# Attention and channel mixing in one kernel: first batch mixed 256 columns wide, its first hidden tile by channel tile, the last product's end in two parts, and a new order of all steps

## The chip, the core and the metric

The kernel runs on one core of one Trainium2 chip. The time is the device time of one execution in microseconds (us), as a median of several runs. Five engines work side by side: PE (TensorE, matrix products; its weight loads are listed apart as PEld), DVE (VectorE), ACT (ScalarE), POOL (GpSimd) and SP (SyncE, which here issues every DMA). Each engine works through its own list of instructions in order and waits on semaphores for the others.

## The reference

Four batches of 768 tokens, 8 heads of 64 channels. Each token attends to its neighbours nearer than 16 and to 24 block summaries (the maximum of the keys, the mean of the values over 32 tokens); the result `x` is mixed over tokens by a product of rank 32 and then goes through two channel products.

```python
scores_l = scale * q @ k^T          # kept where |i - j| < 16
scores_s = scale * q @ k_sum^T + log(32)
a = softmax(concat([scores_l, scores_s]))
x = a @ concat([v, v_sum])          # (4, 768, 512)
u = x + (x^T @ U @ V)^T             # U: 768 x 32, V: 32 x 768
out = u + relu(u @ w_ch1) @ w_ch2   # 512 -> 2048 -> 512
```

## The kernel before, in words

**Front.** Nothing of the channel products can start before batch 0 has been through its attention. Per head the steps are: load keys (`lk`, line 310), queries (`lq`, line 324) and, for two heads at once, values (`lv`, line 345); block maxima on DVE (`K`, line 418) and their copies into the key tile; scores on PE (line 474); masked exponentials on DVE and ACT (lines 499, 509); transposes on PE (line 583) and their copies (line 589); the means of four heads' values on PE (`M`, line 399) and eight copies of them into the value tiles (line 437); the product with the values (line 599); the division on DVE (`N`, lines 627 to 629), which writes `x`. The second `M` (heads 4 to 7) needs the last of the value loads.

Then `x` is mixed. A channel tile is 128 channels (two heads), there are four. `I` (line 642) multiplies `x` by `U` for two channel tiles, as 12 matmuls of 128 columns that use the four 32-column strips of the array in turn; `J` (line 660) adds up the strips by a product with `rep`; both results are copied (lines 655, 668, 670). `G` (`mix_u`) turns three token tiles of one channel tile (three transposes, line 676) and adds the mixed part to the same bank (line 684); `Go` splits the sum into a rounded part on ACT (line 714) and the rest on DVE (line 715). A half is 384 tokens, so there are eight `G`. The hidden tile `f` of half `hf` is `up` (line 1015): 12 matmuls, three for each of four channel tiles.

**Weights.** They come as 64-bit words: a load of 512 KB (`la`, `lb`, `W`, line 802), a scaling on ACT (line 244), three turning steps (POOL line 264, DVE lines 270 and 273), and a split into two parts (ACT line 288, DVE or POOL line 289).

**Main stream.** After the front PE does one group of matmuls after the other: for batch 0 `up` and `down_rows` (line 1037) in turn, for batches 1 to 3 products of half-size blocks (lines 1300, 1396, 1498). The attention of the next batch, the weights and the outputs are laid between these groups. In the batches after the first the exponentials take a way through DRAM before the product with the values (line 613): `s` sends them (line 534), `f` fetches them in four pieces (line 542), `v` loads the values (lines 338, 339).

**Order.** The order of the whole program is the string `PLAN`: words, each one step, with "/" after which the next group of main matmuls follows. What stands before the first "/" is the front (its words begin with a dot). The same order holds on every engine's list, SP's too, and each load's place on SP's list is the place of its word. `.w4` puts four matmuls of 128x120 on a tile of zeros into PE's list (`keep_busy`, line 1139).

**End.** The last stage is 56 pairs of groups of six matmuls of 384 columns (line 1498). After the last group DVE adds the result to `u` (line 1524), and SP sends it (line 1529).

Of the kernel before, what the change touches and what calls it, by code (L numbers as in the profile page):

```python
# [18 lines left out]
P = 128  # L19
BLOCK, WIN = 32, 16  # L20
NB = S // BLOCK
NU = S // P
# [45 lines left out]
    .lu .li .X .w4 .z1 .w4 .lk0 .lk3 .K0 .Xt0 .Kd0 .lq0 .lm .lq3 .lk2 .K3 .S0 .Kd3 .S3 .m .K2  # L68
    .Kp2 .E0.2 .w4 .lq2 .E0.1 .lk1 .F .w4 .lq1 .E1.0 .E7.0 .E6.2 .E1.1 .lv0 .S2 .lv1 .E0.0 .E1.2
    .T1 .K1 .E7.2 .Xt1 .T0 .E7.1 .C0 .E6.1 .lk7 .C1 .E5.2 .E5.0 .E6.0 .Kp1 .E5.1 .lk6 .w4 .T7  # L70
    .S1 .T5 .Xt2 .E2.0 .E4.1 .E2.1 .lq7 .T6 .E3.0 .lq6 .lq4 .M0 .E3.2 .E2.2 .E3.1 .Mo0 .Dp0
    .E4.0 .lk4 .K7 .Kp7 .lk5 .T2 .Bp1 .T3 .C6 .E4.2 .C5 .K6 .Bp0 .C7 .S7 .Kd6 .V1 .C2 .lv2 .T4
    .Dp3 .Xs .Bp3 .V0 .V7 .K4 .E15.2 .lq5 .Kp4 .Dp2 .E14.2 .E15.1 .V6 .C3 .N3 .E15.0 .E14.1 .lv3
    .S6 .Xl .C4 .la0 .S4 .K5 .Qs .E14.0 .Bd2 .Dp1 .E8.1 .V5 .E13.0 l1.0.0 .Kp5 .V4 .E8.2 .N0 .S5
    .E12.2 .E8.0 .V3 .V2 .E11.1 .E13.1 .E12.0 .M1 .lr .E9.0 .E12.1 .E11.2 .T12 .E13.2 .E11.0
    .E9.1 .T8 .T15 .Mo1 .Z0 .C12 .C15 .Dp6 .E10.2 .E10.1 .la1 .Qf .E10.0 .N1 .N2 .T13 .lb0 .T14
    .I0 .Y0.0 .T11 .E9.2 .Bd6 .Dd5 .T9 .Io0 .C11 .Bp4 .Bp7 .C13 .la2 .C8 .Y0.1 .Dp4 .V12 .lb1
    .C9 .V11 .V13 .Y0.2 .J0 .lb2 .V8 .N6 .la4 .Bp5 .T10 a1.0.0 .la3 .V9 .C14 .V14 .Jo0 .C10 q1.0
    .V10 .Dp7 .N4 k1.0 .G0.0 .V15 .G0.1 .lb3 .N5 .Z1 .N7 .Go0.0 a1.0.0 .G1.1 .Go0.1 .I2 .G1.0
    .Y1.0 .Io2 .J2 .z0 .w4 .Y1.1 .Jo2 .G0.2 .W0 .G0.3 .Y1.2 .Go0.2 l1.0.1 .Go0.3 .Z2 .G1.2  # L80
    .Go1.1 .Go1.2 a1.0.0 t2 W0.5 .G1.3 a1.0.0 .Go1.0 t2 .Go1.3 .U0.0 .W1 a1.0.0 / / / t2 c0.4 t2
    t2 a1.0.0 K1.0 .lb4 t2 c0.3 t3 a1.0.0 a1.0.1 w0.0 c1.2 / l1.1.0 w0.1 / x1.1 t3 x0.2 t3 v1.1
    D1 Ka1.0 v1.0 / c1.3 k1.1 S1.0.1 / E1.0.1.0 E1.0.1.1 W0.6 E1.0.1.2 S1.0.0 t3 a1.0.1 t4
    E1.0.0.1 t3 c0.5 E1.0.0.0 D0 K1.1 t5 a1.0.1 E1.0.0.2 a1.0.1 t3 Ka1.1 x0.3 w1.0 / T1.0 x1.2
    q1.1 k1.2 K1.2 / / c1.4 S1.1.0 a1.0.1 t4 / E1.1.0.2 W1.5 U0 S1.1.1 E1.1.0.0 a1.1.0 E1.1.0.1
    W1.6 s1.0 Ka1.2 q1.2 U1 w1.1 E1.1.1.2 E1.1.1.0 t4 a1.0.1 D2 E1.1.1.1 t4 k1.3 Us0 t4 t4 t5 t5
    Us1 f1.0 / c1.5 U4 a1.0.1 a1.0.1 x1.3 / D3 x0.4 a1.0.1 c0.6 / W0.7 t6 S1.2.0 t5 Ba1.1.1 U3
    T1.1 W0.8 E1.2.0.1 Ba1.0.0 E1.2.0.0 a1.1.0 E1.2.0.2 / t5 s1.1 t5 / q1.3 x0.5 W1.7 t6 x1.4
    a1.1.0 D4 S1.2.1 W0.9 Ba1.0.1 E1.2.1.1 K1.3 f1.1 E1.2.1.2 / E1.2.1.0 t6 / t6 c0.7 c0.8 P1.0
    Ba1.1.0 t6 / c1.6 W1.8 N1.0 T1.2 w2.0 t7 Ka1.3 t8 k1.4 / S1.3.0 / s1.2 E1.3.0.2 E1.3.0.0  # L90
    S1.3.1 t6 E1.3.0.1 q1.4 c1.7 P1.1 w2.1 k1.5 x1.5 E1.3.1.0 E1.3.1.1 t7 v1.2 E1.3.1.2 N1.1
    K1.4 x0.6 t7 T1.3 Ka1.4 / Ba1.2.1 / t7 v1.3 c1.8 q1.5 t7 w3.0 t7 / S1.4.0 Ba1.2.0 x1.6 U5
    f1.2 D5 E1.4.0.2 W1.9 R1.0 c0.9 t8 K1.5 x0.7 E1.4.0.0 w3.1 l1.1.1 t8 / Ba1.3.1 W0.10 / /
    E1.4.0.1 W0.11 S1.4.1 Ba1.3.0 E1.4.1.0 E1.4.1.2 E1.4.1.1 a1.1.0 t8 P1.2 t9 s1.3 t9 N1.2 t8
    t8 / / x1.7 T1.4 W1.10 x0.8 q1.6 Ka1.5 c0.10 U6 / a1.1.1 S1.5.0 t10 / f1.3 a1.1.0 E1.5.0.2
    S1.5.1 D7 W1.11 D6 E1.5.0.1 c1.9 t9 t10 E1.5.0.0 t9 t9 c0.11 k1.6 a1.1.1 E1.5.1.1 c1.11 t10
    U7 t11 t9 r1.0 / s1.4 a1.1.0 W0.12 E1.5.1.0 a1.1.1 t10 x1.8 / a1.1.0 g1.0 a1.1.1 E1.5.1.2
    t10 K1.6 Ka1.6 P1.3 N1.3 x0.9 c0.12 / a1.1.1 a1.1.1 M1.0 t10 Mo1.0 c1.10 / J1.0 R1.1 t11 D8
    t11 k1.7 a1.1.1 Jo1.0 x0.10 K1.7 / O1.0.0 W0.13 Us2 x1.9 / t11 t11 Us3 t11 t12 / / f1.4
    c0.13 U2 T1.5 S1.6.0 w5.0 U10 a1.1.1 x0.11 w4.0 / r1.1 t12 E1.6.0.1 q1.7 D10 / E1.6.0.2 v1.4  # L100
    t12 E1.6.0.0 w5.1 a1.1.1 x1.10 W1.12 / S1.6.1 g1.1 U11 W0.14 t13 D9 / U9 W1.13 v1.6 E1.6.1.0
    c1.12 E1.6.1.2 Ba1.4.1 t12 E1.6.1.1 Ka1.7 t12 t13 O1.0.1 t12 w4.1 x0.12 / s1.5 Ba1.4.0 t13
    O1.0.1 O1.0.1 / O1.0.2 P1.4 Us4 t13 x1.11 O1.0.1 t13 c0.14 N1.4 W0.15 / U8 W1.15 T1.6 v1.5
# [87 lines left out]
def body(ctx: ExitStack, tc, q0, q1, k, v, vn, uv, w1, w2, mask, ident, rep, out):  # L191
# [1473 lines left out]
```

## Time and profile before

| | |
|---|---|
| median of 3 runs | 625.55 us (622.32 to 626.25) |
| the profiled execution | 626.52 us, of it the span from first to last instruction 624.3 us |
| PE busy | 610.4 us, 98% of the span |
| DVE, ACT, POOL busy | 72%, 56%, 55% of the span |
[...]
| start of the first `up` / of the first `down_rows` on PE | 50.25 us / 54.55 us |
| end of the last matmul | 620.82 us |

All views are of this one execution; times in them are from the start of its span. A busy PE is not PE at its peak: the ends of matmuls are modelled, so a pause shorter than a matmul does not show as idle.

### The profile page before, as it was taken

To read this page: it belongs to the slowest core of one execution; us is meant where nothing else is said; L and a number is where in the kernel's file an instruction comes from. 1 tells how busy PE (TensorE), PEld (TensorE's weight loads), DVE (VectorE), ACT (ScalarE), POOL (GpSimd) and SP (SyncE) were. 2 spreads that over 40 slices of the span, in tenths; PEclk is the share of its full clock that TensorE was granted. 3 is DMA by queue.
4 is the path that set the end of the run, shared out by engine and by line. 5 is a ranking of instruction groups with operands and counts; after the bars stand their busy time and mean duration, and the time that the engine had idled before them with its cause. 6 is when DMAs were issued, how large, how long until landed. Compare 5 with 4: busy or idle time off the path is not lost.

```text
span 624.3 us, 14694 instructions
## 1 busy us (share of the span) xinstructions
PE 610.4 (98%) x5376; PEld 557.9 (89%) x5376; DVE 446.5 (72%) x1139; ACT 350.9 (56%) x794; POOL 345.6 (55%) x393
## 2 busy tenths in 40 slices
PE   7899999999999999999999999999999999999997
PEld 6679989889987999988887899998888899999997
DVE  5689768678888766779787764776557553579992
ACT  3776666563653666665544556675463556767620
POOL 5377964786666687785345677654333575640000
PEclk9999999999999999999999999999999999999999
DMA  8997998999968678799896786687879645455443
GB/s 222 230 323 246 285 313 258 288 291 325 295 197 281 226 239 262 241 301 300 262 305 181 210 266 203 198 256 237 253 242 311 220 133 168 149 191 203 145 119 126
DMA packets 97559, 148.30 MB, mean 238 GB/s; under 512 B 9680, under 2 KB 67920, under 8 KB 97488
## 3 DMA queue, kind: packets, MB, share of 16 engines
q1 hardware_dynamic: 97488, 147.38, 76.4%
q8 instruction: 42, 0.69, 0.5%
q14 instruction: 29, 0.24, 0.1%
HBM read 104.67 MB, written 42.66 MB: 236 GB/s over the span
## 4 chain that ended last, share of the span: by engine, by line
PE 81%; DMA 12%; SPq 3%; DVE 1%; issue 1%; ACT 1%; POOL 1%; DVEq 0%; ACTq 0%
PE ps_h L1300 25%; PE acc L1396 17%; PE ps_h L1015 10%; PE acc L1037 10%; PE accx L1498 4%; PE accy L1498 3%; PE accz L1498 3%; DMA place<-in_k 2%; PE ps_x L613 2%; DMA dsum<-tmp 2%; PE ps_s L474 2%; PE ps_s L451 2%; DMA there<-squares 2%; SPq L542 1%; DMA whole<-up 1%; DMA place<-in_v 1%
## 5 line engine op out<-in xcount | busy, mean ns | idle before, releaser
L967 POOL TENSOR_TENSOR parts<-whole,parts 128x512 fp32r<-128x512 f32 (+1 forms) x128 | 159.3, 1258 | 77.3 <-ACT parts L963 72.9
L1300 PE MATMUL ps_h<-place,parts 128*128 128x384 f32 x1008 | 179.5, 336 | 0.7 <-DVE x L629 0.7
L1300 PEld LDWEIGHTS ps_h<-place,parts 128*128 128x128 f32 x1008 | 174.3, 188 | 3.0 <-PE ps_h L1300 1.0
L1396 PE MATMUL acc<-gh,parts 128*128 128x256 f32 (+1 forms) x512 | 133.6, 341 | 0.0
L1396 PEld LDWEIGHTS acc<-gh,parts 128*128 128x128 f32 x512 | 88.6, 189 | 12.3 <-issue 1.4
L963 ACT CAST parts<-whole 128x512 fp32r<-128x512 f32 (+1 forms) x144 | 80.8, 581 | 11.9 <-issue 4.6
L1396 PE MATMUL acc<-gl,parts 128*128 128x512 f32 (+1 forms) x256 | 86.5, 338 | 0.0
L1015 PE MATMUL ps_h<-place 128*128 128x384 f32 x384 | 73.9, 341 | 0.4 <-DVE x L695 0.3
L509 ACT ACTIVATE e<-e,neg 128x120 f32<-128x120 f32 x144 | 52.0, 390 | 33.4 <-DVE neg L499 32.3
L1015 PEld LDWEIGHTS ps_h<-place 128*128 128x128 f32 x384 | 67.2, 188 | 3.1 <-DVE x L695 0.7
L1037 PE MATMUL acc<-place,gh 128*128 128x512 f32 x192 | 66.5, 400 | 0.0
L1369 ACT ACTIVATE gh<-place 128x768 fp32r<-128x768 f32 x32 | 27.1, 846 | 62.2 <-PE acc L1396 62.2
L264 POOL TENSOR_SCALAR val<-place 128x512 f32<-128x512 f32 (+1 forms) x33 | 54.1, 1642 | 9.4 <-ACT place L244 4.4
L289 POOL TENSOR_TENSOR place<-val,place 128x512 fp32r<-128x512 f32 x29 | 37.6, 1301 | 29.7 <-ACT place L288 25.2
L1374 DVE SCALAR_TENSOR_TENSOR gl<-place,gh 128x768 fp32r<-128x768 f32 x32 | 38.3, 1196 | 20.3 <-ACT gh L1369 20.2
L1396 PEld LDWEIGHTS acc<-gl,parts 128*128 128x128 f32 x256 | 48.5, 189 | 4.5 <-DVE gl L1374 0.2
L743 POOL TENSOR_TENSOR place<-tmp,place 128x384 fp32r<-128x384 f32 x24 | 27.8, 1163 | 41.0 <-ACT place L739 34.2
L1037 PEld LDWEIGHTS acc<-place,gh 128*128 128x128 f32 x192 | 36.1, 188 | 7.4 <-ACT gh L1027 0.2
L499 DVE CUSTOM_DVE_ANT_0 e<-ps_s,mask_sb 128x120 f32<-128x120 f32 x144 | 35.1, 276 | 6.2 <-PE ps_s L451 4.1
L1027 ACT ACTIVATE gh<-ps_h 128x384 fp32r<-128x384 f32 x32 | 15.7, 489 | 41.0 <-PE ps_h L1015 40.9
L1037 PE MATMUL acc<-place,gl 128*128 128x512 f32 x96 | 37.7, 393 | 0.0
L1329 DVE TENSOR_TENSOR place<-place,ps_h 128x384 f32<-128x384 f32 x24 | 13.3, 554 | 28.7 <-PE ps_h L1300 28.6
(153 smaller groups left out, 1043.4 us busy)
## 6 DMA issues: line engine op xcount, KB each, us to landing
place<-in_w SPq DMA_DIRECT2D x32, 512.0 KB, 5.8
whole<-up SPq DMA_DIRECT2D x24, 512.0 KB, 4.8
there<-squares SPq DMA_DIRECT2D x24, 384.0 KB, 4.8
at<-there SPq DMA_DIRECT2D x96, 96.0 KB, 3.4
whole<-up SPq DMA_DIRECT2D x24, 384.0 KB, 3.9
whole<-down SPq DMA_DIRECT2D x16, 512.0 KB, 5.6
vt<-in_v SPq DMA_DIRECT2D x48, 146.2 KB, 4.2
kt<-in_k SPq DMA_DIRECT2D x24, 288.0 KB, 4.8
```

Of the source, the lines that this page charges most:

```text
L264: nc.gpsimd.tensor_scalar(f32(bits), f32(hi), 0.0, None, ALU.mult)
L289: engine.tensor_tensor(lo, val, f32(hi), ALU.subtract)
L499: nc.vector.tensor_tensor_reduce(out=e[:, u, :], in0=ps[:, i * KC : (i + 1) * KC], in1=mask_sb[:, m, :], scale=-SCALE, scalar=BIG, op0=ALU ...
L509: nc.scalar.activation(e[:, u, :], e[:, u, :], AF.Exp, bias=st.neg[h][:, u : u + 1], scale=-1.0,)
L963: nc.scalar.copy(hi, whole)
L967: (nc.vector if key[0] == "second" else nc.gpsimd).tensor_tensor(lo, whole, f32(hi), ALU.subtract)
L1015: nc.tensor.matmul(ps[:, :NH], w_split[0, f][:, c % 2, part_w, c // 2], ut[c], start=(n == 0), stop=(n == 3 * NC - 1),)
L1037: nc.tensor.matmul(acc[t], gt[:, sl], w_split[1, f][:, part_w], start=(first and j == 0), stop=(last and j == 2),)
L1300: nc.tensor.matmul(ps, a[:, sa, i], b[i][:, sb], start=(first and n == 0), stop=(n == 5), skip_group_check=not first,)
L1374: nc.vector.scalar_tensor_tensor(gl, h, 0.0, f32(gh), ALU.max, ALU.subtract)
L1396: nc.tensor.matmul(place, w[:, part_w, c * P : (c + 1) * P], gt[:, q0:q1], start=(f == 0 and i == 0 and j == 0), stop=(f == NF - 1 and j = ...
L1498: nc.tensor.matmul(ps, w[j][:, sa, c * P : (c + 1) * P], gate[sb], start=fresh and q == 0 and j == 0 and k == 0, stop=q == 3 and j == 1 an ...
```

## The change

Four things are changed.

1. **Mixing, first batch.** `mix_t` takes its columns `w` tiles at a time: for `I` on channel tiles 0 and 1 that is six matmuls of 256 columns in place of twelve of 128. Channel tiles 2 and 3 are mixed one by one (`i`, `j`), so the second group becomes two. `mix_u` is taken apart into the transposes (`G`) and the addition of the mixed part (`g`).
2. **First hidden tile.** `up_channel` does the three matmuls of one channel tile, so that `up` can begin before all channel tiles are ready (`u`).
3. **End.** The last group of the last stage is done first for 256 columns (six matmuls) and then for 128 (six matmuls); DVE's addition and the send are also in two parts.
4. **Order.** `PLAN` is new from its first word to its last. `keep_busy` now does matmuls of 128x512, and the plan has `.w1` six times where it had `.w4` six times.

```diff
-    .lu .li .X .w4 .z1 .w4 .lk0 .lk3 .K0 .Xt0 .Kd0 .lq0 .lm .lq3 .lk2 .K3 .S0 .Kd3 .S3 .m .K2
...
+    .lk1 .lk2 .lq1 .K1 .Kp1 .lk0 .lk3 .w1 .K2 .Kp2 .lm .lq2 .lq3 .K3 .K0 .S1 .Kd3 .Kd0 .lq0 .lu
...
     def mix_t(st, c, n):
 
         ps = bank("ps_m")
-        for i in range(n):
+        w = n if st.b == 0 else 1
+        for i in range(0, n, w):
             for s in range(NU):
                 g = (s + 2 * i) % 4
                 nc.tensor.matmul(
-                    ps[R * g : R * g + R, i * P : (i + 1) * P],
+                    ps[R * g : R * g + R, i * P : (i + w) * P],
                     u_sb[:, s, :],
-                    st.x[:, s, (c + i) * P : (c + i + 1) * P],
+                    st.x[:, s, (c + i) * P : (c + i + w) * P],
...
+    def up_channel(st, f, hf, c):
+
+        uh, ul = st.u[hf]
+        if c == 0:
+            begun[f, hf] = [bank("ps_h"), 0]
+        ps, done = begun[f, hf]
+        assert done == c
+        begun[f, hf][1] = c + 1
+        for n, (part_w, ut) in enumerate(((0, uh), (0, ul), (1, uh))):
+            nc.tensor.matmul(
+                ps[:, :NH],
+                w_split[0, f][:, c % 2, part_w, c // 2],
+                ut[c],
+                start=(c == 0 and n == 0),
+                stop=(c == NC - 1 and n == 2),
+            )
+
     def up(st, hf, f):
...
+        for c in range(begun.get((f, hf), (None, 0))[1], NC):
+            up_channel(st, f, hf, c)
+        return begun[f, hf][0]
...
-            nc.tensor.matmul(ps[:, :KC], spin, spin[:, :KC], start=True, stop=True)
+            nc.tensor.matmul(ps, spin[:, :P], spin, start=True, stop=True)
...
+            last = i == 8 * len(OPS) - 1
...
+            for u0, u1 in ((0, 2), (2, 3)) if last else ((0, 3),):
+                part = slice(u0 * P, u1 * P)
+                for j in range(2):
+                    gate = st.gates[2 * g + j]
+                    for k, (sa, sb) in enumerate(((0, 0), (0, 1), (1, 0))):
+                        nc.tensor.matmul(
+                            ps[:, part],
+                            w[j][:, sa, c * P : (c + 1) * P],
+                            gate[sb][:, part],
...
+                if q == 3:
+                    second_out(st, i, n, c, ps, u0, u1)
```

**Place one: SP's list around the last value loads.** `in_k`, `in_q`, `in_v`, `in_w` are keys, queries, values and weights; each row of values is one load of 293 KB. Before:

```order
L345 DMA place<-in_v 96x780 x4
L310 DMA place<-in_k 128x3x192 x2
L324 DMA x<-in_q 64x384 x6
L310 DMA place<-in_k 128x3x192 x2
L345 DMA place<-in_v 96x780 x2
L324 DMA x<-in_q 64x384 x2
L345 DMA place<-in_v 96x780 x2
L802 DMA place<-in_w 128x1024
```

The same place on SP's list after the change:

```order
L352 DMA place<-in_v 96x780 x4
L331 DMA x<-in_q 64x384 x2
L312 DMA place<-in_k 128x3x192 x3
L331 DMA x<-in_q 64x384 x6
L819 DMA place<-in_w 128x1024
L352 DMA place<-in_v 96x780 x4
L1150 DMA v_there<-place 128x384
```

The last queries now stand ahead of the last four value loads, and so does the first weight load, which stood behind them.

**Place two: PE's list from the second `M` to the first product with the values, and its last rows before `down_rows`.** `ps_n` is `M`, `ps_t` transposes, `ps_m` and `ps_r` the mixing, `ps_x` the values, `ps_u` the turned tiles, `ps_w` the matmuls of zeros, `ps_h` `up`. Before, from the second `M`:

```order
L399 MATMUL ps_n<-place,means_w 32x65 x48
L583 MATMUL ps_t<-ident_sb,gh 120x128 x6
L583 MATMUL ps_t<-ident_sb,gl 120x128 x3
L583 MATMUL ps_t<-ident_sb,gh 120x128 x3
L583 MATMUL ps_t<-ident_sb,gl 120x128 x3
L642 MATMUL ps_m<-x,u_sb 32x128 x12
L583 MATMUL ps_t<-ident_sb,gl 120x128 x3
L583 MATMUL ps_t<-ident_sb,gh 120x128 x3
L599 MATMUL ps_x<-place 64x65 x18
L660 MATMUL ps_r<-t_764,rep_sb 128x256
L599 MATMUL ps_x<-place 64x65 x6
L583 MATMUL ps_t<-ident_sb,gl 120x128 x3
```

After, from the second `M`:

```order
L406 MATMUL ps_n<-place,means_w 32x65 x48
L590 MATMUL ps_t<-ident_sb,gl 120x128 x3
L590 MATMUL ps_t<-ident_sb,gh 120x128 x3
L590 MATMUL ps_t<-ident_sb,gl 120x128 x3
L590 MATMUL ps_t<-ident_sb,gh 120x128 x3
L590 MATMUL ps_t<-ident_sb,gl 120x128 x3
L650 MATMUL ps_m<-x,u_sb 32x256 x6
L606 MATMUL ps_x<-place 64x65 x12
L668 MATMUL ps_r<-t_757,rep_sb 128x256
L606 MATMUL ps_x<-place 64x65 x36
```

Behind the second `M` stand 24 transposes before and 15 after. Before, from the second group of the mixing to `up`:

```order
L642 MATMUL ps_m<-x,u_sb 32x128 x12
L676 MATMUL ps_u<-ident_sb,x 128x128 x3
L684 MATMUL ps_u<-vm_st,t_st 128x384
L660 MATMUL ps_r<-t_921,rep_sb 128x256
L1139 MATMUL ps_w<-kt 128x120 x4
L676 MATMUL ps_u<-ident_sb,x 128x128 x3
L684 MATMUL ps_u<-vm_st,t_st 128x384
```

After, from the same group:

```order
L650 MATMUL ps_m<-x,u_sb 32x128 x12
L684 MATMUL ps_u<-ident_sb,x 128x128 x3
L694 MATMUL ps_u<-vm_st,t_st 128x384
L668 MATMUL ps_r<-t_895,rep_sb 128x128
L668 MATMUL ps_r<-t_897,rep_sb 128x128
L684 MATMUL ps_u<-ident_sb,x 128x128 x3
L1037 MATMUL ps_h<-place 128x384 x6
L694 MATMUL ps_u<-vm_st,t_st 128x384
```

The matmuls of zeros behind the second group are gone, and the first six of `up` stand between two steps of the mixing.

**Place three: SP's list where batch 1 (the second batch) has its last head.** `there<-squares` is `s1.7`, the `at<-there` behind it `f1.7`, `vt<-in_v` is `v1.7`. Before:

```order
L534 DMA there<-squares 128x768
L883 DMA up_110<-val 128x512
L338 DMA vt<-in_v 96x390
L339 DMA vt<-in_v 96x390
L360 DMA place<-in_vn 128x512 x2
L542 DMA at<-there 32x4x192 x4
```

After:

```order
L541 DMA there<-squares 128x768
L900 DMA up_110<-val 128x512
L312 DMA kt<-in_k 128x3x192
L565 DMA rows<-place 128x768
L549 DMA at<-there 32x4x192 x4
L345 DMA vt<-in_v 96x390
L346 DMA vt<-in_v 96x390
```

The two value loads stood ahead of the four fetches and now stand behind them.

## Rows read from the trace of the kernel before

**Rows 1.** Busy time of each engine in three stretches of the span (core 0); behind the five engines stand the granted clock, the share of DMA time and GB/s.

```profile
0.00:33.37 33.37, 26.42 (x468) 22.18 (x468) 20.07 (x123) 18.23 (x54) 14.61 (x46) 1.00 0.92 232
33.37:54.55 21.18, 20.86 (x313) 18.16 (x314) 17.64 (x48) 15.45 (x38) 15.35 (x19) 1.00 0.86 292
...
620.82:624.30 3.48, 0.00 (x0) 0.00 (x0) 0.56 (x1) 0.00 (x0) 0.00 (x0) 0.96 0.32 113
```

**Rows 2.** The chain of work that ended last, in order of time, of the front: start, length, what. A fp32 matmul appears as two.

```profile
25.46 7.87 DMA place<-in_v
...
33.37 1.36 PE ps_n L399 x76
34.73 1.78 PE ps_t L583 x15
36.51 0.79 PE ps_m L642 x24
...
44.84 0.57 PE ps_m L642 x14
45.41 0.14 issue
45.55 0.62 PE ps_m L642 x10
...
46.83 0.51 PE ps_r L660 x2
47.34 0.88 PE ps_w L1139 x8
...
50.25 4.30 PE ps_h L1015 x24
54.55 1.62 PE acc L1037 x7
```

**Rows 3.** The first weight load: its issue on SP's queue (start, length), and in the view of DMA issues its size and time from issue to landing.

```profile
25.92 0.43 SPq L802 DMA_DIRECT2D place<-in_w  x1
...
place<-in_w SPq DMA_DIRECT2D x1, 512.0 KB, 8.4
```

**Rows 4.** Three stretches of 2 us in the front, columns as in Rows 1.

```profile
20.00:22.00 2.00, 1.88 (x78) 1.54 (x66) 0.75 (x3) 0.87 (x4) 0.60 (x2) 1.00 0.65 166
22.00:24.00 2.00, 1.49 (x34) 1.11 (x36) 1.57 (x5) 1.92 (x6) 1.74 (x6) 1.00 0.73 194
24.00:26.00 2.00, 2.00 (x53) 1.69 (x52) 1.17 (x8) 0.64 (x3) 1.69 (x6) 1.00 0.95 262
```

**Rows 5.** DVE in order of time from the last division to the split of the second pair of weights: start, length, what.

```profile
44.15 0.56 DVE L629 TENSOR_TENSOR x<-ps_x,sum 128x384 f32<-128x384 f32 x1
44.62 1.01 DVE L715 TENSOR_TENSOR place<-ps_u,place 128x384 fp32r<-128x384 f32 x2
45.55 1.28 DVE L270 SCALAR_TENSOR_TENSOR val<-place,val 128x512 int32<-128x512 int32 x2
47.78 0.43 DVE L670 TENSOR_TENSOR t_st<-ps_r,t_st 64x256 fp32r<-64x256 f32 x1 [0.94 <-ACT t_st L668]
48.30 0.69 DVE L289 TENSOR_TENSOR place<-val,place 128x512 fp32r<-128x512 f32 x1
...
53.16 0.55 DVE L1028 SCALAR_TENSOR_TENSOR gl<-ps_h,gh 128x384 fp32r<-128x384 f32 x1
53.63 1.55 DVE L289 TENSOR_TENSOR place<-val,place 128x512 fp32r<-128x512 f32 x2
```

**Rows 6.** The three longest of what PE waited for between 56 and 620 us: us in total, times, the longest.

```profile
PE ps_m L642 <- DVE x L629: 0.8, 2, 0.6
PE ps_h L1300 <- DVE x L629: 0.7, 1, 0.7
PE ps_x L613 <- DMA whole<-up: 0.4, 1, 0.4
```

**Rows 7.** The end: the last piece of PE in the chain, DVE's last addition and SP's last four issues in order of time, and the send's time from issue to landing.

```profile
612.45 8.37 PE accy L1498 x48
...
620.84 0.56 DVE o L1524
...
612.02 9.74 SPq L1529 DMA_DIRECT2D out_t<-o  x4
...
out_t<-o SPq DMA_DIRECT2D x1, 192.0 KB, 1.9
```

**Rows 8.** Matmuls of 256 columns in the third batch, in order of time: start, length to the modelled end, what.

```profile
444.35 0.40 PE L1396 MATMUL acc<-gh,parts 128*128 128x256 f32 x2
444.59 0.28 PE L1396 MATMUL acc<-gl,parts 128*128 128x256 f32 x1
```

**Rows 9.** The second batch's last head: SP's send, the second value load, the four fetches and PE's product with the values, in order of time; and the time from issue to landing of line 339 over the program (24 loads).

```profile
176.65 0.34 SPq L534 DMA_DIRECT2D there<-squares  x1
...
179.14 0.44 SPq L339 DMA_DIRECT2D vt<-in_v  x1
...
181.32 1.88 SPq L542 DMA_DIRECT2D at<-there  x4
...
187.69 0.89 PE L613 MATMUL ps_x<-vt,at 120*32 120x65 f32 x48
...
DMA to landing us min/median/max: 2.3/4.4/7.2
```

More of the change, by code (lines that the diff above doesn't have):

```diff
@@ L320, in load_q, with load_half_q @@
         st.qt[h] = qd0[h] if st.b == 0 else qz[h % 2].rearrange("p u q -> p (u q)")[:, :NH]
[L321 to L324 removed]
+        for t in range(2):
+            load_half_q(st, h, t, nc.sync)
+    def load_half_q(st, h, t, by):
+        if st.b == 0:
+            st.qt[h] = qd0[h]
+        flat = (q0, q1)[t][st.b, :, h].rearrange("d u q -> d (u q)")
+        i = flat.shape[1] // 2 - NH // 2
+        by.dma_start(out=st.qt[h][64 * t : 64 * t + 64], in_=flat[:, i : i + NH])
     def load_qk(st, h):
@@ L683, in mix_u, with add_mixed @@
             )
+    def add_mixed(st, hf, c):
         nc.tensor.matmul(
-            ps[:, :NH], st.t_st[:, c], vm_st[:, hf * NH : (hf + 1) * NH], start=False, stop=True
-        )
-        st.ps_u[hf, c] = ps
+            st.ps_u[hf, c][:, :NH],
+            st.t_st[:, c],
+            vm_st[:, hf * NH : (hf + 1) * NH],
+            start=False,
+            stop=True,
+        )
+    def mix_u(st, hf, c):
+        turn_tiles(st, hf, c)
+        add_mixed(st, hf, c)
     def add_rows(st, hf, c, kept):
@@ L1082, in body @@
     raw_uv = weight_place(0, 2, I32)[:, : 4 * NU * R]
[L1084 removed]
+    spin = kv.tile([P, KTW], F32, name="kt")[:, : 4 * P]
     nc.gpsimd.memset(spin, 0.0)
@@ L1494, in second_phase @@
             ps = banks[to, c]
-            for j in range(2):
-                gate = st.gates[2 * g + j]
-                for k, (sa, sb) in enumerate(((0, 0), (0, 1), (1, 0))):
-                    nc.tensor.matmul(
-                        ps,
-                        w[j][:, sa, c * P : (c + 1) * P],
-                        gate[sb],
-                        start=fresh and q == 0 and j == 0 and k == 0,
-                        stop=q == 3 and j == 1 and k == 2,
-                        skip_group_check=not fresh,
-                    )
-            if q == 3:
-                second_out(st, i, n, c, ps)
+            last = i == 8 * len(OPS) - 1
+            last_to = n == len(OPS) - 1 and c == 1
+            for u0, u1 in ((0, 2), (2, 3)) if last else ((0, 3),):
[7 more added lines that the diff above has]
+                            gate[sb][:, part],
+                            start=fresh and q == 0 and j == 0 and k == 0,
+                            stop=(q == 3 or last_to and q == 2) and j == 1 and k == 2 or last,
+                            skip_group_check=last or not fresh,
+                        )
+                if q == 3:
+                    second_out(st, i, n, c, ps, u0, u1)
             yield
```

278 lines of the change are left out of this document (135 added, 143 removed).

## The prediction

> **What bounds the kernel now.** I read first the busy time by stretch [rows 1]. From 33.37 to 54.55 us PE is busy for 20.86 of 21.18 us, and in the whole span it lacks only 14 us (624.3 less the 610.4 of the table). Nearly half of these, 6.95 us, lie before 33.37 us, where PE waits for loads and also fills time with matmuls of zeros; 3.5 us lie behind the last matmul. So three places can give time: the front, the waits inside the main stream, the end. [...]
>
> Then I read the chain of work that ended last [rows 2]. The reader is to see one change of owner: up to 33.37 us the chain is a DMA, the last value load (issued at 25.46, landed 7.87 later), and the DMA share is 0.92 [rows 1]. From 33.37 on the chain is PE alone, with one pause named issue (0.14 us) in the rows shown, down to the first `up` at 50.25 and the first `down_rows` at 54.55. So the front is two lengths in series: the loads up to the last value, then 21.18 us of PE work. Cutting PE work ahead of the last value load is worth nothing; cutting it behind is worth its full time, if DVE keeps up.
>
> **Front, behind the second `M`.** By the two orders:
> - Transposes: 24 stand there before, 15 after. Fifteen took 1.78 us, 0.119 each [rows 2], so nine moved ahead are -1.07 us. What hides them is the idle time of PE before 33.37; if the exponentials that they read come late, they cost the same again.
> - The matmuls of zeros at 47.34 are gone from there: -0.88. Their cover is now work of `up`, of which the total (24 matmuls, 4.30 us) is unchanged. The early matmuls of `up` need the first weights split by then, which the new order does before the second `M`.
> - The first group of the mixing took 0.79 us as 24 passes of 128 columns, three rounds on each strip of the array. With 256 columns strips 0 and 1 get two matmuls each and strips 2 and 3 one, so the longest strip has four rounds of 128: 4/3 of 0.79, +0.26. If the group is bound by the number of its matmuls it halves instead: -0.39. No row has the new shape; I take +0.26, since the 36.51 row is as long as its columns on one strip ask for (three rounds of two passes, 0.13 each, beside 0.119 for a transpose of 128 columns).
> - The second group took 0.57 + 0.62 with 0.14 of waiting between, 1.33. Two single tiles have four rounds too, 1.05, and transposes stand where the wait was: -0.28. Its second step (the piece of 0.51 at 46.83 in [rows 2]) becomes two products: between 0 and +0.5, I take +0.1.
>
> Sum: -1.07 - 0.88 + 0.26 - 0.28 + 0.1 = -1.9 us (bounds -2.5 and -1.1).
>
> DVE must follow. Before, it goes from the end of the last division (44.71) to the end of the weight split (55.18) in 10.47 us, of which 0.94 is a wait [rows 5]. After, the same stretch has eight remainders (0.5 each, 4.0), four turning steps (1.28 a pair, 2.6), one block maximum that was later (0.55, its keys must have landed, or all of these stand behind it), two small remainders of the mixing (0.3 each), one `gl` (0.5), and the split (1.55): 9.8. The split of the first weights (0.69) is gone from it. The last division itself ends some 1.3 us earlier behind the second `M`: nine transposes less (1.07), a longer first group (0.26), and one turned tile that stood ahead of the last product with the values and now follows it (three transposes and a matmul of 384 columns, 3 x 0.119 + 0.174 = 0.53, an estimate from [rows 2, 7]). So DVE allows 1.3 + 0.7 = 2.0. Neither engine can give much more than PE's sum, and this is the first place where the gain can stop.
>
> **Front, ahead of the second `M`.** A weight load of 512 KB now stands ahead of the last four value loads. In the trace of before it was issued at 25.92 and landed 8.4 later, at 34.3 [rows 3], 1.0 us behind the last value. So by 34.3 all that the new order wants landed had landed: +1.0 us at the same rate. Against it: between 20 and 24 us the DMA moved 166 and 194 GB/s where 262 is seen right behind [rows 4]. That is a gap of (262 - 180) x 4 us = 0.33 MB, or 1.25 us at 262. The queries that were issued there singly now stand together with larger loads, so it may close: lower bound 1.0 - 1.25 = -0.25. Upper bound: 0.524 MB at the mean rate of 232 GB/s [rows 1] with none of it hidden, +2.3. I take +0.6, nearest to the measured landing with part of the gap closed. The other reordered loads (64-bit mixing matrices behind the first keys) leave the bytes up to the last value as they were.
>
> The scaling of that weight stands on ACT ahead of some twenty exponentials. If it waits for the load, they wait too; they have until the last value lands, so this is counted in the +2.3.
>
> **End.** The last group of six takes 6 x 0.174 = 1.04 us (8.37 for 48) [rows 7]. Matmuls of 256 columns are 0.120 apart (444.35 to 444.59 for two) [rows 8], so the first part is 0.72. The 128-column part has no row. From below: the step from 384 to 256 columns is 0.054, so 0.066 each, 0.40 in all. From above: the matmuls of zeros are 128x120 in plain fp32, 0.88 for four of them [rows 2], 0.22 each, 1.32 in all. I take 0.09 each, 0.54, near the straight line because the operands are of the same kind: PE +0.22 (+0.08 to +1.0). [...]
>
> Behind the last matmul DVE then adds 128 columns instead of 384: 0.56 for 384 [rows 7], 0.43 for 256 of another kind [rows 5], so about 0.3: -0.26. The send of 192 KB landed in 1.9 us [rows 7]; a third of the bytes saves between 0 and 0.5 (131 KB at the 262 GB/s of [rows 4]), I take 0.2. The first part's addition and issue (0.4 + 0.34) end before the second's addition does. Sum: +0.22 - 0.26 - 0.2 = -0.25 (bounds -0.7 and +0.75).
>
> **Main stream.** No instruction is added or removed there, but all stand in a new order. PE's waits between 56 and 620 us are short; the longest single ones are 0.7 and 0.6 [rows 6], all six together are 2.9. The new order keeps none of their places. One new place looks worse (below), so I take 0, with bounds -2.5 (most waits go) and +4.
>
> **Sum.** -1.9 + 0.6 - 0.25 + 0 = -1.55. On the profiled execution's own 626.52 us that is 625.0. This execution lies 0.97 above the median of the runs shown (625.55), so for a median: 624.0.
>
> **The rivals.**
> - *More is gained:* the gap in the DMA closes fully (-0.25 in place of +0.6), the end gives its -0.7, and the waits on a division (0.8 and 0.7) go: -1.9 - 0.25 - 0.7 - 1.5 = -4.35, that is 621.2 for a median. For it: DMA share 0.65 and 0.73 in the gap. Against it: DVE's 9.8 us.
> - *Nothing is gained:* the last value is 2.3 us late, which eats the -1.9; with the end 625.7. For it: the load's 8.4 us to landing. Against it: all of it had landed 1.0 us behind the last value.
> - *Slower:* in the second batch's last head the value loads now stand on SP's list behind the fetch, which waits until the sent squares have landed. Before, from send to PE's use there were 11.04 us (176.65 to 187.69), with the values issued at 179.14. After, they are issued behind the four fetches: 181.32 + 1.88 is 6.55 us behind the send, and with 2 x 0.44 of issue 7.4. They land 4.4 later in the median, 7.2 at most [rows 9]: 11.8 or 14.6 against 11.04, if PE is at its place as early as before. Price 0.8 in the median, 3.6 at most; it decides from 1.55 on, that is if they take over 5.2 us to land. At its most: 626.52 - 1.55 + 3.6 = 628.6, for a median 627.6. A longer distance in the new order speaks against it.
>
> **How the numbers follow.** Chances: the forecast 0.45 (622.5 to 625.2 by itself), more gained 0.2, nothing gained 0.2, slower 0.15. The range 619.5 to 628.0 takes in the second and third case and the nearer part of the last; what lies outside is a main stream that beats or misses its bounds. About 1% (6.3 us) is what a measurement of this kernel can tell from no change. Faster by that needs all bounds on the good side and more (below 619.3): 0.07. Slower by that (above 631.8) needs several waits like the one named: 0.06. Within 1%: 0.87.
>
> **What would show it.** In the profile after: the second `M` on PE near 34.0; the first `down_rows` 19.3 us behind the second `M`'s start, near 53.2, with no matmuls of zeros behind it; DVE without a pause between the last division and the split; the 128-column matmuls at the end 0.09 apart and the span ending 3.0 us behind the last of them; PE's waits in the main stream at 1 to 5 us. The forecast is wrong if the second `M` starts past 36, or if a wait of over 2 us shows at any line of the main stream.

## The result and the profile after

The changed kernel takes 628.83 us (median of 18 runs, 626.11 to 634.01), the kernel before 623.75 us in the same comparison (18 runs, 621.78 to 631.67). The ratio is 1.0081, 95% interval 1.0060 to 1.0103: 5.1 us slower, where 1.55 us faster was forecast, and above the upper end of the range (628.0). The prediction counts anything within 1% as no change, and 0.8% lies within that, but the interval does not hold 1. The ratios in this document are taken over the fast runs alone and are printed as they were recorded; they differ by up to 0.0016 from the quotients of the two medians given beside them. The profiled execution took 628.88 us with a span of 626.9, against 626.52 and 624.3 before.

Where the 2.6 us between the two spans lie is read at two marks on PE that both kernels have, the first `down_rows` and the first `accx` (last stage). PE in order of time after the change, with the second `M` as a third mark: start, length, what.

```profile
33.51 1.59 PE L406 MATMUL ps_n<-place,means_w 96*32 96x65 f32 x96
...
52.99 0.39 PE L1062 MATMUL acc<-place,gh 128*128 128x512 f32 x1
...
562.45 2.24 PE L1535 MATMUL accx<-gate,parts 128*128 128x384 f32 x12
```

The two marks in the same view of before:

```profile
54.39 0.39 PE L1037 MATMUL acc<-place,gh 128*128 128x512 f32 x1
...
560.09 2.24 PE L1498 MATMUL accx<-gate,parts 128*128 128x384 f32 x12
```

So, between these two executions, the front won 1.40 us, the main stream between the marks went from 505.70 to 509.46 and lost 3.76, and what follows lost 0.24. What PE waited for between 50 and 627 us (us in total, times, longest), against [rows 6]:

```profile
PE ps_h L1333 <- DVE o L1085: 2.7, 1, 2.7
PE acc L1429 <- DVE gl L1407: 2.3, 2, 1.8
PE ps_x L620 <- DMA whole<-down: 0.3, 1, 0.3
PE ps_h L1037 <- DVE place L732: 0.3, 1, 0.3
```

One wait of 2.7 us stands where the longest before was 0.7. The second row is new too: two waits, the longer 1.8, for the remainder `gl` that DVE computes. Line 1085 is in `finish_rows` (word `o`): PE turns the first batch's finished rows into a bank (`ps_o`), DVE adds `u` into a buffer `o`, and SP sends that. The chain of waits around it (start, length, what):

```profile
236.20 0.78 PE ps_s L481 x24
236.97 0.27 PE ps_o L1081
237.25 0.17 SPq L312
237.41 0.05 issue
237.46 4.21 DMA whole<-up
241.67 0.56 DVE o L1085
242.23 0.04 issue
242.27 0.95 PE ps_h L1333 x2
```

The chain names a weight load (`whole`) behind a load of keys (line 312) for which SP's queue had stood. DVE and POOL in order of time show another candidate:

```profile
236.04 0.48 POOL L375 TENSOR_TENSOR stage<-stage 128x128 f32<-128x128 f32 x1
...
236.87 0.98 DVE L536 STREAM_TRANSPOSE squares<-e 128x768 f32<-128x768 f32 x1 [0.59 <-ACT e L516]
...
238.82 2.49 POOL L984 TENSOR_TENSOR parts<-whole,parts 128x512 fp32r<-128x512 f32 x2
241.25 0.10 POOL L380 MEMSET vsum<- 128x1 f32 x1
241.31 0.32 POOL L381 TENSOR_TENSOR vsum<-stage 128x64 f32<-128x64 f32 x1
241.66 1.49 DVE L1085 TENSOR_TENSOR o<-ps_o,place 128x384 f32<-128x384 f32 x3 [3.81 <-DMA whole<-up]
```

POOL's sum at line 381 ends at 241.63 and the weight load lands at 241.67, 0.04 apart; DVE starts at 241.66. `stage` (values being summed, words `l` to load and `a` for each step) and `o` take turns in the same eight buffers, so the sum can be what DVE waited for; by the times alone either event fits. The first two experiments tell them apart.

The clock fell twice, each time behind a pause. Busy time by stretch, columns as in [rows 1]:

```profile
18.00:20.00 2.00, 0.21 (x16) 0.14 (x12) 0.10 (x1) 0.37 (x2) 0.00 (x0) 1.00 1.10 233
20.00:22.00 2.00, 2.00 (x84) 1.83 (x87) 0.95 (x6) 0.14 (x2) 0.00 (x0) 0.62 1.11 310
22.00:24.00 2.00, 2.00 (x29) 1.70 (x26) 0.80 (x3) 1.40 (x5) 1.65 (x4) 0.52 1.03 223
242.00:244.00 2.00, 1.73 (x6) 1.73 (x7) 2.00 (x5) 0.00 (x0) 0.89 (x3) 0.59 1.12 252
244.00:246.00 2.00, 2.00 (x8) 2.00 (x7) 1.40 (x8) 0.00 (x0) 0.00 (x0) 0.56 0.67 172
```

In the front PE was idle for 1.8 us before the first values, and the granted clock then stood at 0.50 from 20.5 to 23.5 us; behind the wait of 2.7 us it did so again, from 242.5 to 245.5. In the trace of before its mean over the span is 1.000. Over 242 to 246 us the clock lacks (1 - 0.59) x 2 + (1 - 0.56) x 2 = 1.7 us of PE's work: from 244 to 246 us PE did 8 matmuls of line 1333 at 0.56, from 246 to 248 us 14 at 1.00. So the wait cost, by estimate, up to 2.7 + 1.7 = 4.4 us.

The end: DVE's last additions and SP's sends in order of time.

```profile
622.16 0.55 DVE L1561 TENSOR_TENSOR o<-x,accy 128x384 f32<-128x384 f32 x1 [6.28 <-PE accy L1535]
622.75 2.00 SPq L1566 DMA_DIRECT2D out_t<-o  x3
623.49 0.62 DVE L1561 TENSOR_TENSOR o<-x,accy 128x256 f32<-128x256 f32 x2 [0.78 <-PE accy L1535]
```

Both parts of the last addition stand at 623.49, behind the last of all twelve matmuls; the first part did not start behind its own six.

### The profile page after: what moved, and what is told of

It is laid out like the page before. It is cut to its first block, busy times and chain, and to the rows that moved or that the text cites. A ratio compares the mean times of both kernels' runs of the same rounds, so it can differ in the third digit from the quotient of the medians.

```text
span 626.9 us, 14613 instructions
## 1 busy us (share of the span) xinstructions
PE 609.9 (97%) x5336; PEld 553.2 (88%) x5336; DVE 436.7 (70%) x1141; ACT 350.0 (56%) x796; POOL 341.9 (55%) x393
## 4 chain that ended last, share of the span: by engine, by line
PE 87%; DMA 7%; SPq 3%; DVE 1%; POOL 1%; issue 1%; ACT 0%; DVEq 0%; POOLq 0%; ACTq 0%
PE ps_h L1333 27%; PE acc L1429 16%; PE acc L1062 11%; PE ps_h L1037 11%; PE accx L1535 4%; PE ps_x L620 3%; PE accy L1535 3%; PE accz L1535 3%; PE ps_s L481 2%; DMA whole<-down 2%; PE ps_s L458 2%; DMA place<-in_v 1%; DMA halfA<-parts 1%; PE ps_x L606 1%; DMA rows<-place 1%; PE ps_t L590 1%
## 5 line engine op out<-in xcount | busy, mean ns | idle before, releaser
L984 POOL TENSOR_TENSOR parts<-whole,parts 128x512 fp32r<-128x512 f32 (+1 forms) x128 | 157.2, 1241 | 107.1 <-ACT parts L980 95.2
L1333 PE MATMUL ps_h<-place,parts 128*128 128x384 f32 x1008 | 182.3, 338 | 2.7 <-DVE o L1085 2.7
L980 ACT CAST parts<-whole 128x512 fp32r<-128x512 f32 (+1 forms) x144 | 80.0, 580 | 19.5 <-DMA halfA<-parts 6.9
L266 POOL TENSOR_SCALAR val<-place 128x512 f32<-128x512 f32 (+1 forms) x33 | 52.6, 1603 | 16.4 <-ACT place L246 11.5
L291 POOL TENSOR_TENSOR place<-val,place 128x512 fp32r<-128x512 f32 x29 | 39.6, 1376 | 26.1 <-ACT place L290 23.1
L1407 DVE SCALAR_TENSOR_TENSOR gl<-place,gh 128x768 fp32r<-128x768 f32 x32 | 35.5, 1113 | 17.3 <-ACT gh L1402 17.1
L760 POOL TENSOR_TENSOR place<-tmp,place 128x384 fp32r<-128x384 f32 x24 | 26.2, 1101 | 21.5 <-ACT place L756 21.4
L1053 DVE SCALAR_TENSOR_TENSOR gl<-ps_h,gh 128x384 fp32r<-128x384 f32 x32 | 17.7, 554 | 25.2 <-ACT gh L1052 25.0
```

What stands on the lines that cost most here:

```text
L266: nc.gpsimd.tensor_scalar(f32(bits), f32(hi), 0.0, None, ALU.mult)
L291: engine.tensor_tensor(lo, val, f32(hi), ALU.subtract)
L980: nc.scalar.copy(hi, whole)
L984: (nc.vector if key[0] == "second" else nc.gpsimd).tensor_tensor(lo, whole, f32(hi), ALU.subtract)
L1333: nc.tensor.matmul(ps, a[:, sa, i], b[i][:, sb], start=(first and n == 0), stop=(n == 5), skip_group_check=not first,)
L1407: nc.vector.scalar_tensor_tensor(gl, h, 0.0, f32(gh), ALU.max, ALU.subtract)
```

## The experiments

All are variants of the changed kernel unless they say otherwise; their lines stand 5 or 6 lower than there (line 1085 is 1080, line 381 is 376, line 1333 is 1328). The kernel before ran beside them each time.

**One word moved: POOL's sum (`a_ahead`).**

```diff
-    f2.0 a2.1.0
+    f2.0 a2.1.0 a2.1.0
...
-    F p1 a2.1.0
+    F p1
```

> The changed kernel with one word moved: the third of the steps that sum the third batch's first values of heads 4 to 7 on POOL stands right behind the second, some ten words earlier. In the trace after the change PE waits 2.72 us for DVE's addition at line 1085, and the granted clock is 0.5 for about 3.4 us behind that wait. Theory POOL: the addition waits for the buffer that this summing step releases (POOL ends it at 241.63, DVE starts at 241.66). Then the wait at line 1085 falls below 0.5 us, the clock stays at 1.00 there, and the time falls by 2.7 + 1.7 = 4.4, less what shows up behind it: 3.5 to 4.5 us below the changed kernel, a median near 624.7. Theory SP: the wait comes from SP's queue, which stands for 6.1 us at the load of keys (line 312) with the weight loads behind it. Then a wait of over 2 us stays at the same place and the median stays within 1 us of 628.8. Theory many small things: the one wait goes, others take its place, and the median falls by less than 1.5 us.

623.11 us (12 runs) against 625.63 before, ratio 0.9975 (0.9941 to 1.0008). From the 1.0081 of the changed kernel this is 1.1% or 6.6 us, more than theory POOL's 3.5 to 4.5, though the two intervals allow anything from 3.3 us on. POOL and DVE in order of time:

```profile
235.87 0.32 POOL L376 TENSOR_TENSOR vsum<-stage 128x64 f32<-128x64 f32 x1
...
237.03 1.45 DVE L1080 TENSOR_TENSOR o<-ps_o,place 128x384 f32<-128x384 f32 x3
...
238.49 2.54 POOL L979 TENSOR_TENSOR parts<-whole,parts 128x512 fp32r<-128x512 f32 x2
```

The sum now runs ahead of the weight splits, DVE's addition starts without a wait right behind what stood ahead of it, PE's wait at that line is gone, and the granted clock has no dip in the main stream (mean over the span 0.999, against 0.995 in the changed kernel's trace). Nor was that one lucky execution: the mean granted clock of every run is on record, and 10 of these 12 runs have 0.999 or more; of the 12 runs of `k_behind`, which has the same front and keeps the wait, 3 do.

**One word moved: SP's load of keys (`k_behind`).**

```diff
-    k2.5 p0 a2.0.1
+    p0 a2.0.1
...
-    S2.2 a2.0.1
+    S2.2 k2.5 a2.0.1
```

> The changed kernel with one word moved: the load of the keys of the third batch's head 5 stands behind the scores of head 2, whose buffer it needs, as in the kernel before. Theory SP: the DMA engines no longer stand still for 3 us near 236, the weight loads behind land 5 us earlier, the 2.7 us wait at line 1085 goes, and the median falls by about 4 us to 624.7. Theory POOL: SP's wait of 6.1 us at line 312 goes, but PE still waits 2 to 3 us for line 1085 with the clock at 0.5 behind it, and the median is 628 to 629.5. Theory many small things: 0.5 to 1.5 us less.

628.40 us against 625.63, ratio 1.0053 (1.0022 to 1.0085). POOL, DVE and PE in order of time:

```profile
240.12 0.31 POOL L376 TENSOR_TENSOR vsum<-stage 128x64 f32<-128x64 f32 x1
...
240.47 1.49 DVE L1080 TENSOR_TENSOR o<-ps_o,place 128x384 f32<-128x384 f32 x3 [3.79 <-POOL vsum L376]
...
241.08 5.13 PE L1328 MATMUL ps_h<-place,parts 128*128 128x384 f32 x19 [2.70 <-DVE o L1080]
```

SP's queue no longer stands at the keys. The weight load behind them was issued at 234.94 and took 3.8 us to land, so it had landed 1.7 us ahead of DVE's start; yet the wait is the same, and now the view names POOL. Theory SP falls; the chain of the changed kernel had named the wrong one of two events that came 0.04 us apart.

**One weight split fewer ahead of POOL's sum (`a_half`).**

```diff
-    F p1 a2.1.0
+    F a2.1.0 p1
```

> The changed kernel with the third summing step of the third batch's values moved ahead by one word only, so that on POOL it stands one weight split (1.25 us in the changed profile) earlier than in the changed kernel and two later than where the wait vanished. Theory POOL, by dose: PE waits 2.7 - 1.25 = 1.4 to 1.5 us for DVE's addition at the same line, and the median is 626 to 627.5. If the wait had another cause that the larger move happened to remove, it stays at 2.7 or goes to nothing.

626.41 us against 623.91, ratio 1.0040 (1.0008 to 1.0072). POOL, DVE and PE in order of time:

```profile
242.67 0.32 POOL L376 TENSOR_TENSOR vsum<-stage 128x64 f32<-128x64 f32 x1
242.94 1.27 POOL L979 TENSOR_TENSOR parts<-whole,parts 128x512 fp32r<-128x512 f32 x1
...
243.02 1.49 DVE L1080 TENSOR_TENSOR o<-ps_o,place 128x384 f32<-128x384 f32 x3 [2.58 <-POOL vsum L376]
...
243.63 2.55 PE L1328 MATMUL ps_h<-place,parts 128*128 128x384 f32 x13 [1.48 <-DVE o L1080]
```

One weight split (1.27 us) fewer ahead of the sum, and PE's wait is 1.48 in place of 2.7, as theory POOL had it by dose (1.4 to 1.5); the median is in its range too. The clock stayed at 1.00 behind this shorter wait.

**Filling PE's pause in the front (`fill`).**

```diff
-    .F .M0
+    .F .w1 .w1 .M0
```

> The changed kernel with two more matmuls of zeros (128x512, 1.04 us each by the changed profile) ahead of the first product for the means of values. After the change PE waits 1.8 us there for values, the granted clock is 0.5 from 20.5 to 23.7, and PE's list is then full up to the second such product at 33.58, although the last values landed at 31.86. Theory clock: without the pause the clock stays at 1.00, about 1.6 us of PE's time comes back, less up to 0.4 by which the first product starts late; the second product stands near 32.3, and all behind it is 1.2 us earlier (median near 627.6, as long as the main stream keeps its waits). Rival: the exponentials on DVE and ACT or the last values set the second product, it stays within 0.5 us of 33.6, and nothing is gained.

627.71 us against 625.63, ratio 1.0049 (1.0023 to 1.0076). The second `M` stands at 32.60. That is 0.9 ahead of the changed kernel's 33.51, but `k_behind` and `front_only`, without the filling, have it at 32.53 and 32.54: in their executions the clock did not fall in the front. `one_end` (below), where it did not fall either, has 33.26. So the fall can have cost the changed kernel's profiled execution between 0.2 and 1.0 us, and the filling shows no gain of its own. In this trace the wait at line 1080 is 2.71 us again, and this time the clock did not fall behind it:

```profile
242.00:244.00 2.00, 2.00 (x14) 2.00 (x13) 1.95 (x8) 0.56 (x2) 0.00 (x0) 1.00 0.59 113
244.00:246.00 2.00, 2.00 (x13) 2.00 (x12) 1.98 (x8) 1.73 (x5) 0.44 (x1) 1.00 0.91 358
```

**The new front alone (`front_only`).** Up to the first "/" the words of the changed kernel, then those of before; the few words that one front has and the other not stand right behind it. The end is in one part.

```diff
-            last = i == 8 * len(OPS) - 1
+            last = False
```

> The changed kernel's front (its words up to the first group of main products, 256-wide mixing, first hidden tile by channel tile, matmuls of zeros of 512 columns) with the order of the kernel before for all that follows, and the last product in one part. Theory main stream: the front is 1.4 us faster (first down_rows near 53.15 in place of 54.55) and the order behind keeps its few waits, so the time is 1 to 1.8 us below the kernel before, a median near 622.3 against 623.7. Rival: the front hands over a worse state (loads of the next batch and weights that stand later), then the gain of 1.4 is given back within the main stream and the median is 623.5 or above.

621.92 us against 625.63, ratio 0.9955 (0.9924 to 0.9985): by the ratio 2.8 us faster than before, where 1 to 1.8 were expected. It is the lowest ratio of all, though the intervals overlap. The first `down_rows` stands at 51.23, the main stream takes 504.45.

**Everything mended (`mended`).** `a_ahead` and `k_behind` together, and the first part's addition put out between the parts:

```diff
                 if q == 3:
                     second_out(st, i, n, c, ps, u0, u1)
+                while last and late and u0 == 0:
+                    finish_late()
```

> The changed kernel with the summing step of the third batch moved ahead, the load of keys of head 5 moved behind the scores of head 2, and the addition of the last product's first part put out between the two parts' matmuls, so that PE signals behind the first six and not only behind all twelve. Theory POOL alone in the main stream: moving the keys adds nothing to the earlier run of the summing step (623.1 us, ratio 0.9975 to the kernel before). Theory that SP's blocked queue was a second cause hidden behind the first: 1 us or more below that. The end: the first part's addition now starts behind its own matmuls, 0.6 us ahead of the last matmul's end and not behind it, the last send is issued some 0.4 earlier, and the span ends 3.0 us behind the last matmul where it ended 3.47 behind it. Together: 622.5, ratio 0.995 to 0.998.

623.91 us against 624.87, ratio 0.9979 (0.9945 to 1.0013): no better than `a_ahead` alone. The keys' place adds nothing that can be measured, and the gain expected at the end does not show.

**The new front, 128-wide mixing and the end put out between (`best`).** `front_only` with the end of `mended`, and

```diff
-        w = n if st.b == 0 else 1
+        w = 1
```

> The changed kernel's front with the order of before for all that follows, the end in two parts with the first part's addition put out between, and the first group of the mixing with 128 columns in place of 256 (twelve matmuls in place of six). If the group is as long as the longest strip, it takes 0.79 us here against 0.99 in the changed kernel, 0.2 off the front; if it is bound by the number of matmuls, it takes longer than 0.99. The end gives 0.4. So 0.6 below the earlier run of this front alone (621.9, ratio 0.9955): 621.3, ratio 0.993 to 0.996; a rival in which the end gives nothing stays at 621.9.

622.77 us against 624.87, ratio 0.9963 (0.9931 to 0.9995): not below `front_only`, where 0.6 us less were expected. The end of this trace, DVE and PE in order of time:

```profile
615.05 0.42 DVE L1558 TENSOR_TENSOR o<-x,accy 128x256 f32<-128x256 f32 x1 [0.16 <-PE accy L1529]
...
615.52 0.89 PE L1529 MATMUL accy<-gate,parts 128*128 128x128 f32 x6 [0.51 <-DVE o L1558]
616.45 0.29 DVE L1558 TENSOR_TENSOR o<-x,accy 128x128 f32<-128x128 f32 x1 [0.98 <-PE accy L1529]
```

The first part's addition now starts behind its own matmuls, but the second part's matmuls wait 0.51 us until DVE has read the bank that both parts share. The division took more ahead of the last matmul than it gave behind it: from the first `accx` to the end of the span it is 64.7 us here and 64.2 in `front_only`, which has the end in one part.

**The kernel before once more (`before_again`).**

> The kernel before, unchanged, for a second trace of it. If the front's length scatters from run to run (in five traces of the new front the first down_rows starts between 51.2 and 53.0), it scatters here as well: the second product for the means and the first down_rows (54.4 in the first trace) move by 0.5 to 1.5 us, and the distance between the two stays near 21.2. If the front of the first trace was typical, 54.4 comes again within 0.3.

621.97 us (one run). Its first `down_rows` stands at 52.43, 2.0 us earlier than in the first trace of the same kernel, and its main stream takes 503.54 where the first took 505.70: two executions of one kernel differ by 2 us in each. The distance from the second `M` to the first `down_rows` did not stay near 21.2 as expected: by the view of PE it is 20.3 (32.09 to 52.43), where the first trace has 21.0 (33.37 to 54.39). The granted clock stood at 0.50 from 8 to 14 us in this front, which was the shorter one even so, and the longest wait of its main stream is 1.6 us.

**The word moved, the end in one part (`one_end`).** `a_ahead` with `last = False`.

> The changed kernel with the summing step moved all the way ahead and the last product in one part, as before the change. From the start of the last group of matmuls to the last landing the kernel before takes 3.69 us, the changed one 4.00, the one with the first addition put out between 4.16. If the division of the end costs what these traces show, 3.7 comes again and 0.3 us is won, less than the medians can tell: 622.8 on the chip of the earlier run, ratio 0.995 to 0.9985. If the division was a gain, it is slower than 0.9975 by 0.3 us and the stretch is over 4.0.

624.17 us against 623.91, ratio 0.9996 (0.9967 to 1.0026). The medians can't tell it from `a_ahead`. The stretch from the last group's start to the last landing is 3.7 us again, as the traces had it; the 0.3 us can be seen there and not in the medians.

**The new front with 128-wide mixing (`front_128`).** `front_only` with `w = 1`.

> The changed kernel's front with the order of before for all that follows, the last product in one part, and the first group of the mixing in twelve matmuls of 128 columns in place of six of 256. Four rounds of 0.22 us become six of 0.11, the group is 0.2 us shorter, and from the second product for the means to the first down_rows there are 18.5 us where the same front with 256 columns had 18.7. The median falls by no more than that: ratio 0.994 to 0.997. If the first down_rows is set by DVE behind the last division, the 0.2 vanish there and 18.7 stays.

622.23 us against 623.91, ratio 0.9967 (0.9937 to 0.9996). From the start of the second `M` to the first `down_rows` it is 19.0 us here (32.83 to 51.87) and 18.7 in `front_only`, but here the second `M` itself took 2.02 us in place of 1.59, with a pause in its middle for which the profile names no releaser. From its end (33.72 + 1.12 here, 32.61 + 1.52 there, in the chains) to the `down_rows` of the chain (52.03, 51.39) it is 17.19 and 17.26. So 0.07 of the 0.2 us arrive; the one wait of PE that is left behind the second `M` in both, 0.3 us for DVE's remainder at the start of `up`, is where the rest can go. In both chains what stands right ahead of `up` is ACT and DVE, for 6.5 us here and 4.3 there, and not PE; that fits the case in which DVE sets the end of the front. The width is worth nothing that can be measured.

The marks of all traces, read as in the first fence (main stream: first `accx` less first `down_rows`):

| kernel | order of the main stream | first `down_rows` | first `accx` | main stream | PE's wait for `o` |
|---|---|---|---|---|---|
| before | before | 54.39 | 560.09 | 505.70 | none |
| before_again | before | 52.43 | 555.97 | 503.54 | none |
| front_only | before | 51.23 | 555.68 | 504.45 | none |
| front_128 | before | 51.87 | 557.54 | 505.67 | none |
| best | before | 51.09 | 554.63 | 503.54 | none |
| after | new | 52.99 | 562.45 | 509.46 | 2.7 |
| k_behind | new | 51.83 | 562.51 | 510.68 | 2.7 |
| fill | new | 51.74 | 560.43 | 508.69 | 2.7 |
| a_half | new, half moved | 55.56 | 562.19 | 506.63 | 1.5 |
| a_ahead | new, moved | 52.18 | 556.81 | 504.63 | none |
| mended | new, moved | 57.48 | 562.98 | 505.50 | none |
| one_end | new, moved | 52.10 | 558.54 | 506.44 | none |

The means are 504.6 with the old order, 509.6 with the wait of 2.7, 505.5 with the word moved. The trace of `mended` is of the slowest of its 12 runs (629.56); without it the last mean is 505.5 as well.

## Why the prediction was wrong, point by point

**Main stream: the step that failed.** "No instruction is added or removed there ... so I take 0, with bounds -2.5 (most waits go) and +4." By the means it is +5.0 us, beyond the upper bound; the two executions compared first have +3.76. 4.1 of the 5.0 are one wait and what follows it (509.6 to 505.5 when one word moves): 2.7 of waiting, and in two of the three traces the clock at 0.5 behind it. The trace without that fall (`fill`) has the shortest main stream of the three. The forecast had named a wait of over 2 us in the main stream as what would make it wrong, and that is what came. It looked for the new wait on SP's list and in the values; it was a buffer that changes hands on POOL, and no view of the trace of before can show that, only the new order of POOL and DVE. The 0.9 us that are left between the moved word and the old order are less than two executions of one kernel differ by; whether they are real stays open. One candidate was not tested: waits of PE's `acc` for DVE's `gl`, as in the second row of the list of waits above, stand in all seven traces with the new order (0.5 to 2.3 us in total) and in none of the five with the old.

**The named rival for slower did not come.** After the change the values of the second batch's last head were issued behind the fetches as said, 182.60 and 183.07 against a send at 174.66, and PE used them at 186.08 with no wait for them in the list. They landed 2.7 us after their issue, where the rival needed more than 5.2.

**Front behind the second `M`: right in size, and DVE now sets it.** 19.3 us from its start to the first `down_rows` were forecast. It was 19.5 (33.51 to 52.99) in the changed kernel, 18.7 in `front_only`, against 21.0 and 20.3 in the two traces of before. (The items of the forecast's own sum bound it by -2.6 and -1.5, and not by the -2.5 and -1.1 that it states; nothing hangs on that.) The first group of the mixing went from 0.79 to 0.99 us; +0.26 was forecast by the longest strip. This is the chain of the front after, answering to [rows 2]:

```profile
33.58 1.52 PE ps_n L406 x96
35.10 1.78 PE ps_t L590 x15
36.88 0.99 PE ps_m L650 x12
...
43.96 0.49 ACT place L731
...
46.01 1.20 DVE val L272 x2
...
48.48 1.30 DVE val L275 x2
...
50.42 2.72 PE ps_h L1037 x14
53.15 2.17 PE acc L1062 x9
```

The reader is to see a second change of owner. Before, PE alone was the chain down to `down_rows`; now it leaves PE at 43.9 and comes back at 50.42, and between the two it is ACT once and then DVE. So the place that the forecast named as the first where the gain can stop is where it stops: of 0.2 us less work for PE ahead of it, 0.07 arrived (`front_128`).

DVE went from the end of the last division (43.81 + 0.56) to the end of the weight split (52.70 + 1.29) in 9.6, with one pause of 0.16 in it; 9.8 was forecast.

**Front ahead of the second `M`: right in size by luck, wrong in its owner.** Near 34.0 was forecast, 33.5 came. The gap in the DMA closed in part: from 20 to 24 us it moved 310 and 223 GB/s, against 166 and 194 [rows 4]. But the chain from 19.89 to 33.58 is PE alone: the second `M` stood behind PE's own list, which had run at a granted clock of 0.50 from 20.5 to 23.5, and not behind the last value load. In the traces of this front where the clock stayed at 1.00 and PE had no stop, it started at 32.5 to 33.3. In the second trace of before it started at 32.09, so here the two kernels differ by less than two executions of one of them, and the +0.6 is not confirmed.

**End: wrong in sign.** -0.25 was forecast, +0.24 came. All twelve traces agree on it: from the first `accx` to the end of the span it is 64.2 to 64.3 us with the end in one part (five traces), 64.5 with two parts (five), and 64.6 to 64.7 with the addition put out between (two). DVE's 0.26 and the 0.2 of the send were to come from a first part that is added while PE does the second. It isn't: in the changed kernel the additions are put out after all twelve matmuls, and PE signals only behind the last one. Put out in between, it makes PE wait for DVE at the shared bank, 0.5 us in both traces (`best`, `mended`). PE's own term was mis-sized a little: the 128-column matmuls are 0.11 to 0.12 apart (six in 0.89, the last with its modelled end of 0.27), where 0.09 was taken.

**The base.** The forecast was put 0.97 below its own sum, for a median of three runs. The median over 18 lay 2.8 below the profiled execution, and the second trace of before shows why one trace is a weak base: 2 us in the front, 2 in the main stream.

**What it sums to.** Front -1.4 (the two executions compared first), main stream +5.0 (the means) and end +0.2 give +3.8 us; the medians say 5.1, with an interval of 3.7 to 6.4. The difference of 1.3 us is not explained. Front and old order together (`front_only`) are 2.8 us faster than before by the ratio and beat both kernels.

## What to carry to other kernels

Here a change that only reordered work was not neutral for buffers that several engines share in turn: the main stream took 509.6 us, and 505.5 with one word moved. For each buffer that a new order hands over, look up on every engine's list what stands ahead of the step that releases it; here two weight splits on POOL (2.49 us) stood right ahead of a sum of 0.32 us, and PE waited 2.7 us, in two of three traces with the clock at 0.5 behind it. When a view names a releaser and another event lies as close to it as here (0.04 us), move each by itself before you believe it. Dividing the last step did not shorten the end here: 64.2 to 64.3 us in one part, 64.5 with two parts and one signal behind both, 64.6 to 64.7 with a signal for each part and one bank for both. Parts with a bank each were not tried.

## What the runs showed of the hardware

The fall of the clock behind a pause is not certain. Behind the same wait of 2.7 us it fell to 0.5 in two traces (`after`, `k_behind`) and stayed at 1.00 in a third (`fill`). In the front it fell behind PE's wait of 1.8 us for the first values (`after`) and stayed at 1.00 behind one of 1.7 (`front_128`). So in these traces the length of the pause alone does not decide it.

In two of the twelve traces (`a_half`, `mended`) PE stopped for 3.1 and 4.1 us in the front with nothing that it waited for, and its clock was at 0.5 behind that. From PE's waits of `a_half` between 16 and 30 us:

```profile
PE ps_s L476 <- issue: 3.1, 1, 3.1
```

The DMA queues that carry instructions between 14 and 20.5 us (packets, MB, share), first of `a_half`, then of the changed kernel:

```profile
q14 instruction: 1, 0.01, 0.6%
```

```profile
q8 instruction: 1, 0.02, 1.2%
q14 instruction: 1, 0.01, 0.5%
```

The ten traces without such a stop have a packet of the instruction queue q8 in that stretch, these two have none. That PE's instructions came late there is the author's guess; nothing was run to test it. The stops fit the late first `down_rows` of these two (55.56 and 57.48). Whether they are also part of the scatter of the medians is not shown.
